# A fused Sinkhorn attention and SwiGLU kernel: a written order on PE, two-bank drains at the start, attention pieces between FFN steps, and unread matmuls in PE's gaps

## The chip, the cores and the metric

The kernel runs on one core of a Trainium2 chip. The metric is the device time of one execution in microseconds (us); smaller is better. The profile gives the span from the first to the last instruction, which is about 2 us shorter than the device time of the same run. Where two traces are compared, spans are used; where two kernels are compared, device times.

PE is the matmul engine, PEld its weight loads, DVE is VectorE, ACT is ScalarE, POOL is GpSimd. A drain is a copy that takes a matmul's result out of its PSUM bank. An unread matmul is one whose result nobody uses. The granted clock is the share of PE's full clock that the throttle allowed. Where several copies are quoted per copy, that is their busy time divided by their number: neighbouring records overlap, so the mean record on the page is longer.

## The reference

```python
B, H, S, D, n_blocks = 4, 8, 768, 64, 8          # block C = 96
P = sort_net                                       # (B, H, 8, 8)
for _ in range(5):                                 # Sinkhorn
    P = exp(P - max(P)); P /= P.sum(-1) ; P /= P.sum(-2)
k_sorted = einsum('bhij,bhjcd->bhicd', P, k_blocks)   # mix the 8 blocks
v_sorted = einsum('bhij,bhjcd->bhicd', P, v_blocks)
attn = softmax(q_block @ k_sorted.T / 8)           # 96 x 96 per block
x = (attn @ v_sorted)                              # as (3072 tokens, 512)
out = (silu(x @ w_gate) * (x @ w_val)) @ w_out     # 512 -> 1536 -> 512
```

Inputs and output are fp32; the kernel computes in bf16 with fp32 accumulation.

## The kernel before

A batch has eight attention units (two halves of the sequence times four pairs of heads). FFN works on a half of a batch (384 tokens) at a time, which I call a half-step: 12 gate and 12 value steps of 4 matmuls each, and an output projection of 3 x 12 matmuls. The parts that matter (cuts marked `# ...`):

```python
psum = ctx.enter_context(tc.tile_pool(name="psum", bufs=3, space=PSUM))   # one bank per tile

for it in range(5):                                # Sinkhorn: ScalarE and VectorE in turn
    nc.scalar.activation(p_sb, p_sb, AF.Exp)
    nc.vector.reduce_sum(...); nc.vector.reciprocal(...); nc.vector.tensor_mul(...)   # rows, columns
# ... the mix: lmix on VectorE, 16 small matmuls, products with masks

def emit_kq(b):                                    # mixes k, passes q: 12 chunks of 8 columns
    for cb in range(C // 8):
        tp = psum.tile([128, 8, 64], FP32, name="tkq", tag="att")
        for lc in range(8):
            for two in range(2):
                nc.tensor.matmul(tp[two * D:(two + 1) * D, lc, :], lhsT=nat[:, cb * 8 + lc, :],
                                 rhs=rm[:, two, :], start=True, stop=True)
        drain(dst[:, :, ts(cb, 8)], tp.transpose([0, 2, 1]))    # VectorE and ScalarE in turn

def emit_vch(pair):                                # transposes v's two free dimensions
    for s in range(4):                             # ... cs is the s-th quarter of the columns
        eng = nc.gpsimd if pair else nc.vector
        eng.tensor_copy(vch[:, :, cs], nat[:, cs, :].transpose([0, 2, 1]))

emit_att(0)
for b in range(B):
    if b + 1 < B:
        emit_att(b + 1)                            # all eight units of the next batch
    emit_gv(b, 0); emit_gv(b, 1); emit_out(b, 0); emit_out(b, 1)
```

The framework's scheduler orders the instructions of each engine and may mix these stages.

The softmax here doesn't subtract the row's maximum and nothing guards it: scores larger than these inputs give would overflow.

## Time and profile before

285.65 us (median of 4 runs, 285.48 to 286.93). The profiled execution took 287.63 us, so the spans and times of its trace below lie about 2 us above those of a median run.

| what | before |
|---|---|
| span | 285.9 us |
| PE's first matmul | 13.6 us |
| FFN dense from about | 46 us |
| PE busy | 257.2 us (90%) |
| granted clock, 36 to 49 us | 0.50 |

Lines of the profile's page, kernel before: busy times; then three rows of the span in 40 equal slices (7.15 us each), where a digit is a busy share, or granted PE clock, in tenths; then the chain of work that ended last.

```profile
PE 257.2 (90%) x2600; PEld 152.7 (53%) x2608; DVE 178.9 (63%) x383; ACT 121.7 (43%) x246; POOL 39.1 (14%) x51
...
PE   0077799969999999999999999999999999999993
...
ACT  2036745437633215976534215764332134343211
...
PEclk9999955979999999999999999999999999999999
...
PE 82%; DVE 11%; ACT 3%; issue 2%; ACTq 0%
```

PE bounds the kernel, but a busy digit doesn't say how much a busy PE gets done: the two 5s in the clock row are slices in which it is busy at least 90% of the time, at half speed. The timeline of PE in that stretch (start, duration, engine, line, operation, output<-inputs, shape, count) shows it:

```profile
36.09 0.51 PE L288 MATMUL g_ps<-xt,wg_sb 128*128 128x384 bf16 x1
36.39 0.52 PE L297 MATMUL v_ps<-xt,wv_sb 128*128 128x384 bf16 x1
36.71 0.52 PE L288 MATMUL g_ps<-xt,wg_sb 128*128 128x384 bf16 x1
37.30 0.50 PE L255 MATMUL x_ps<-ident,st 96*128 96x96 bf16 x4
```

Two starts of 384-column matmuls are 0.30 to 0.32 us apart; later in the trace they are 0.163 us apart (0.65 us for a step of four). The records overlap (0.51 us long, 0.30 us apart), so starts are compared throughout this text, not durations.

### The profile page before, as it was taken

How to read it: one execution, taken by the hardware profiler on the slowest of the kernel's cores; microseconds unless marked ns; L12 is line 12 of the kernel's file. 1: busy time of each engine (PE TensorE's matmuls, PEld its weight loads, DVE VectorE, ACT ScalarE, POOL GpSimd, SP SyncE). 2: the span in 40 equal slices, each digit the busy share in tenths (PEclk: the TensorE clock that was granted, in tenths of full speed). 3: DMA queues.
4: the chain of work that ended last, by engine and by line, in shares of the span. 5: the costliest groups of instructions: out<-in, count | busy, mean ns of one | idle time of the engine just before them, and what ended most of it. 6: DMA issues, size and time to landing. Idle time of an engine off the chain costs nothing.

```text
span 285.9 us, 6221 instructions
## 1 busy us (share of the span) xinstructions
PE 257.2 (90%) x2600; PEld 152.7 (53%) x2608; DVE 178.9 (63%) x383; ACT 121.7 (43%) x246; POOL 39.1 (14%) x51
## 2 busy tenths in 40 slices
PE   0077799969999999999999999999999999999993
PEld 0066555746655446666655446666555445555441
DVE  6798746937988205789988304699885018888300
ACT  2036745437633215976534215764332134343211
POOL 8557421029500000000000000000000000000000
PEclk9999955979999999999999999999999999999999
DMA  6999999999100122000000122000000220000021
GB/s 99 198 203 197 200 213 204 220 214 214 38 0 1 39 110 76 2 2 0 3 0 2 38 110 76 2 2 2 0 0 2 111 102 10 0 0 3 37 110 73
DMA packets 13659, 20.84 MB, mean 73 GB/s; under 512 B 1088, under 2 KB 8768, under 8 KB 13632
## 3 DMA queue, kind: packets, MB, share of 16 engines
q0 software_dynamic: 10128, 14.16, 28.2%
q1 hardware_dynamic: 3504, 6.30, 5.8%
q8 instruction: 20, 0.33, 0.4%
q14 instruction: 7, 0.06, 0.1%
HBM read 28.32 MB, written 6.29 MB: 121 GB/s over the span
## 4 chain that ended last, share of the span: by engine, by line
PE 82%; DVE 11%; ACT 3%; issue 2%; ACTq 0%
PE v_ps L297 22%; PE g_ps L288 22%; PE o_ps L308 22%; PE av_ps L245 4%; PE qk L230 4%; PE tkq L193 3%; PE x_ps L255 3%; PE tv L214 3%; DVE kqt L180 2%; DVE vch L204 1%; DVE st L251 1%; ACT vt L182 1%; DVE vt L180 1%; ACT th_sb L291 1%; DVE colred L136 0%
## 5 line engine op out<-in xcount | busy, mean ns | idle before, releaser
L288 PE MATMUL g_ps<-xt,wg_sb 128*128 128x384 bf16 x384 | 84.8, 331 | 0.2 <-DVE h L299 0.2
L297 PE MATMUL v_ps<-xt,wv_sb 128*128 128x384 bf16 x384 | 82.1, 331 | 0.0
L291 ACT ACTIVATE th_sb<-g_ps 128x384 bf16<-128x384 f32 x96 | 47.1, 491 | 63.2 <-PE g_ps L288 62.6
L293 DVE SCALAR_TENSOR_TENSOR gs_sb<-th_sb,g_ps 128x384 bf16<-128x384 bf16 x96 | 52.9, 551 | 26.9 <-ACT th_sb L291 20.9
L308 PE MATMUL o_ps<-wo_sb,h 128*128 128x512 bf16 x280 | 62.4, 379 | 0.4
L299 DVE SCALAR_TENSOR_TENSOR h<-v_ps,gs_sb 128x384 bf16<-128x384 f32 x96 | 53.1, 553 | 9.0 <-PE v_ps L297 0.8
L297 PEld LDWEIGHTS <-wv_sb 128*128 128x128 bf16 x384 | 36.8, 98 | 24.5 <-issue 0.8
L288 PEld LDWEIGHTS <-wg_sb 128*128 128x128 bf16 x384 | 36.2, 99 | 23.5 <-issue 2.3
L308 PEld LDWEIGHTS <-h 128*128 128x128 bf16 x288 | 28.2, 98 | 33.6
L180 DVE CAST kqt<-tkq 128x512 bf16<-128x512 f32 x24 | 15.9, 688 | 33.9 <-PE tkq L193 33.9
L311 ACT COPY o_sb<-o_ps 128x512 f32<-128x512 f32 x24 | 14.1, 586 | 51.4 <-PE o_ps L308 51.4
L235 ACT ACTIVATE er<-qk 96x384 bf16<-96x384 f32 x64 | 27.1, 487 | 12.2 <-PE qk L230 12.2
L193 PE MATMUL tkq<-rmix,kq 128*64 128x64 bf16 x768 | 20.3, 212 | 5.5 <-issue 2.5
L193 PEld LDWEIGHTS <-kq 128*64 128x64 bf16 x768 | 17.7, 126 | 8.9 <-issue 7.9
L251 DVE TENSOR_TENSOR st<-av_ps,r_sb 96x512 bf16<-96x512 f32 x32 | 21.9, 684 | 0.8
L182 ACT CAST kqt<-tkq 128x512 bf16<-128x512 f32 x24 | 14.1, 586 | 15.7 <-PE tkq L193 15.6
L230 PE MATMUL qk<-kqt 64*128 64x96 bf16 x256 | 14.0, 217 | 1.9 <-DVE kqt L180 1.4
L245 PE MATMUL av_ps<-vt,er 96*128 96x65 bf16 x256 | 14.9, 202 | 0.2 <-ACT vt L182 0.2
L180 DVE CAST vt<-tv 96x512 bf16<-96x512 f32 x16 | 12.2, 785 | 2.7 <-PE tv L214 2.5
L182 ACT CAST vt<-tv 96x512 bf16<-96x512 f32 x16 | 12.5, 787 | 2.1 <-PE tv L214 1.8
L214 PE MATMUL tv<-vmix,vch 128*128 128x128 bf16 x128 | 12.4, 236 | 1.0 <-DVE vt L180 0.3
L255 PEld LDWEIGHTS <-st 96*128 96x128 bf16 x128 | 7.6, 101 | 10.5 <-DVE st L251 9.1
(43 smaller groups left out, 123.0 us busy)
## 6 DMA issues: line engine op xcount, KB each, us to landing
out_dram<-o_sb SPq DMA_DIRECT2D x24, 256.0 KB, 2.0
v<-in_v_dram POOLq DMA_DIRECT2D x8, 384.0 KB, 13.1
kq<-in_k_dram POOLq DMA_DIRECT2D x6, 384.0 KB, 11.6
kq<-in_q_dram POOLq DMA_DIRECT2D x6, 384.0 KB, 12.1
wg_sb<-in_moe_w_gate_dram POOLq DMA_DIRECT2D x6, 256.0 KB, 11.8
wv_sb<-in_moe_w_val_dram POOLq DMA_DIRECT2D x6, 256.0 KB, 11.1
wo_sb<-in_moe_w_out_dram POOLq DMA_DIRECT2D x1, 1536.0 KB, 18.9
kq<-in_k_dram POOLq DMA_DIRECT2D x4, 192.0 KB, 5.6
```

Source lines behind the costliest of these rows:

```text
L180: nc.vector.tensor_copy(dst, src)
L182: nc.scalar.copy(dst, src)
L193: nc.tensor.matmul(tp[two * D:(two + 1) * D, lc, :], lhsT=nat[:, cb * 8 + lc, :], rhs=rm[:, two, :], start=True, stop=True)
L230: nc.tensor.matmul(pss[two][:, i4, :], lhsT=flat[lo:lo + D, at:at + 128], rhs=kqt[lo:lo + D, 1, g, i, :], start=True, stop=True)
L235: nc.scalar.activation(e[:, 0:4 * C], pss[two][0:C].rearrange("p a c -> p (a c)"), AF.Exp, scale=scale)
L245: nc.tensor.matmul(av[:, two, i4, :], lhsT=es[two][:, i4 * C:i4 * C + 128], rhs=vt[:, 2 * g + two, half * 4 + i4, :], start=True, stop=True)
L288: nc.tensor.matmul(g_ps, lhsT=wg_sb[:, kc, ts(m, 128)], rhs=xt[:, kc, :], start=(kc == 0), stop=(kc == NKC - 1))
L291: nc.scalar.activation(th_sb, g_ps, AF.Tanh, scale=0.5)
L293: nc.vector.scalar_tensor_tensor(gs_sb, th_sb, 1.0, g_ps, op0=ALU.add, op1=ALU.mult)
L297: nc.tensor.matmul(v_ps, lhsT=wv_sb[:, kc, ts(m, 128)], rhs=xt[:, kc, :], start=(kc == 0), stop=(kc == NKC - 1))
L299: nc.vector.scalar_tensor_tensor(h_w[:, m, :], v_ps, 0.5, gs_sb, op0=ALU.mult, op1=ALU.mult)
L308: nc.tensor.matmul(o_ps, lhsT=h_w[:, m, ts(t3, 128)], rhs=wo_sb[:, m, :], start=(m == 0), stop=(m == NFC - 1))
```

## The change

The intent: reach dense FFN work sooner, keep PE's clock up, and hide the attention of later batches between FFN steps. The diff is long (an almost new body); this is its core, with cuts marked `...`. First the order: the instructions of four engines stand as written in the start, those of PE and GpSimd for the rest.

```diff
+    man = tc.manual_schedule(engines={ET.PE, ET.Pool, ET.DVE, ET.Activation})
...
+    def copy_v(eng, pair, rows, s, n=4):
+        cs = slice(s * (C // n), (s + 1) * (C // n))
+        dst = vch3[rows, :, cs]
+        src = v_tiles[pair][rows, cs, :]
+        if eng is nc.scalar:
+            eng.copy(dst.transpose([0, 2, 1]), src)
+        else:
+            eng.tensor_copy(dst, src.transpose([0, 2, 1]))
...
     for it in range(N_ITER):
         nc.scalar.activation(p_sb, p_sb, AF.Exp)
...
+        if it == 2:
+            copy_v(nc.scalar, 0, lowr, 0, 8)
+            copy_v(nc.scalar, 0, lowr, 1, 8)
+        if it == 3:
+            copy_v(nc.scalar, 0, lowr, 2, 8)
+            copy_v(nc.scalar, 0, lowr, 3, 8)
...
+    for s in range(4, 8):
+        copy_v(nc.scalar, 0, lowr, s, 8)
```

Then the start on two-bank tiles, with unread matmuls (`fill`) between its four units:

```diff
+    for cb in range(6):                            # was 12 chunks of one bank
+        tp = pair_tile("tkq").rearrange("p (l n) -> p l n", n=2 * GI)
+        for lc in range(16):
...
+        drain("sv"[cb % 2], dst[:, :, ts(cb, 16)], tp.transpose([0, 2, 1]))
...
+    def fill(n):
+        warm(pair_tile("warm_ps")[:, 0:512], slice(0, 128), kqts[0][:, 0:512], n)
+
+    for u in range(4):
+        qk_wide(u)
+        fill(2)
+        if u >= 1:
+            av(0, u - 1, "pair")
+            fill(1)
...
```

Then the FFN stage: `merge` puts one attention piece after about every FFN step, in the order of the list, and an output projection comes one half-step after its gate and value steps. All k/q and v drains of this stage are on ScalarE ("s"), the drains of the transposes on VectorE ("v").

```diff
+    def kqs(b):
+        return [(0.34, lambda cb=cb: kq_chunk(b, cb, "s", "att")) for cb in range(12)]
...
+    merge(ffn(0), units(0, range(4, 8)) + kqs(1))
+    merge(ffn(1), [(0.28, lambda db=db: v_chunk(1, db, "s", "att")) for db in range(8)]
+          + units(1, range(4)))
...
+    merge(ffn(2), units(1, range(4, 8)) + kqs(2))
...
+    merge(ffn(4), units(2, range(4, 8)) + kqs(3))
+    merge(ffn(5), units(3, range(4)))
+    merge(ffn(6), units(3, range(4, 8)))
+    merge(ffn(7), [])
```

## The prediction

> **What bounds the kernel before.** PE: the chain of waits gives it 82% of the span. But there are two regimes.
>
> Steady state: the output projections of the four batches begin at 94.5, 159.0, 218.5 and 266.1 us (chain, in order of time). Warm rates from the timeline: gate or value step of 4 matmuls 0.65 us, output step of 4 0.87 us, qk 0.27, av 0.27, transpose 0.20 per unit, a k/q chunk 0.35. One batch of FFN is 48 x 0.65 + 18 x 0.87 = 46.9 us; the last period is 47.6 us, the one before 59.5 us for about 57 us of work. So it is already 96-99% dense; reordering it can win little.
>
> Start: the work done before 94.5 us is, at warm rates, about 31 us of gate/value plus 27 us of attention for batches 0 and 1, and PE's first matmul comes at 13.6 us. That would end at about 71 us: some 23 us are lost. Where (windows): one-bank drains and vch copies on VectorE alternate with PE from 14 to 33 us; a serial chain qk-exp-av-st-transpose of 2.5 us per unit at granted clock 0.50 from 36 to 49 us (a 384-column matmul takes 0.32 us instead of 0.16); an issue gap of 2.5 us at 57.4 us. The Trainium skill, "TensorE: Matmul & The Clock Gate", Part 1, says that the clock halves after an idle window and needs about 3.4 us of activity to return; this trace agrees (0.50 in 36-48 us, 1.00 from 51 us).
>
> **The change** loads only batch 0's v first, fuses the last Sinkhorn multiply with the mix, copies v on ScalarE inside Sinkhorn's gaps, drains two banks per instruction, runs only four of eight units before FFN, fills gaps with 25 unread 512-column matmuls, then spreads the rest between FFN steps.
>
> **Cost of the new start.** Sinkhorn rounds take 1.76 us: mix ready near 12.3 us, v products from about 13 us. Two-bank drains, estimated from the slope between 384 and 512 columns (ScalarE 478 to 586 ns): about 1.0 us ScalarE, 1.25 us VectorE; five on each, so k/q is ready at about 21.5 us (PE, cold at first, takes as long). Four units at about 2 us plus 2 us of pipeline end: first dense gate step at about 31.5 us.
>
> **The rest.** FFN 187.7 us, 28 units x 0.74 = 20.7, 36 k/q chunks = 12.4, v products about 5.8: 226.6 us. Stalls 6 us (2-3%): ScalarE now makes all k/q and v drains; half-step 3 has 16 v drains of 0.79 us beside tanh, locally more than PE's time; VectorE is tight in half-step 0. End as before, about 4 us. Sum: 31.5 + 226.6 + 6 + 4 = 268 us. Weights are no limit: 4.3 MB at about 200 GB/s, landed near 25 us.
>
> **Prediction: 268 us, 80% range 261 to 276.** Faster by over 2%: 0.93; within 2%: 0.06; slower: 0.01.
>
> **What would show it.** First gate matmul near 31.5 us (before: dense from 46); the slices' PEclk row without a 5 after 20 us; PE idle below 3% from there on; two-bank drains about 1.0/1.25 us; projections of the last half ending near 264 us.
>
> **What would make it wrong.** Clock lost in spite of the filling (10 us more); fillers or buffer rotation on the chain themselves (3 us); ScalarE copies delaying Sinkhorn; PE stalled behind ScalarE in half-steps 1 and 3 beyond 6 us; another issue gap while the DMA queues are full; or a shorter pipeline of four units (262 us).

## More of the kernel before

Note `emit_vch`: on VectorE, columns are innermost, so it writes runs of 24 neighbouring values.

The copy that will matter, from the groups of the profile by shape, kernel before: VectorE moves 1536 values per partition in 1.49 us.

```profile
L204 DVE COPY vch<-v 128x1536 bf16<-128x1536 bf16 x4 | 6.0, 1490 | 0.0
```

## The result

The changed kernel takes 303.99 us (median of 4 runs, 301.75 to 304.37) against 285.65 us: slower, by a ratio of 1.0615 (95% interval 1.0555 to 1.0675). A ratio here is the mean time of one kernel's fast runs over that of the other's of the same rounds, so it is not quite the ratio of the medians.

| what | before | after |
|---|---|---|
| span | 285.9 us | 302.5 us |
| v products begin | 25.6 us | 37.4 us |
| first dense gate step | about 46 us | 58.5 us |
| from there to the end | about 240 us | 244.0 us |
| ScalarE busy | 121.7 us | 159.2 us |

The page's lines, changed kernel, as before (slices of 7.56 us); the last is a group of the page's costliest: busy us and mean ns after the bar.

```profile
PE 257.4 (85%) x2675; PEld 146.3 (48%) x2697; DVE 154.6 (51%) x345; ACT 159.2 (53%) x261; POOL 40.8 (13%) x42
...
PE   0500087989999999999999999999999999999994
...
ACT  4999954454665544446499526355533244333321
...
PEclk9999996999999999999999999999999999999999
...
PE 77%; ACT 12%; DVE 6%; issue 2%; DMA 2%; ACTq 0%; POOLq 0%
...
L112 ACT COPY vch<-v 64x768 bf16<-64x768 bf16 x8 | 31.1, 4328 | 0.2 <-DMA v<-in_v_dram 0.2
```

The reader should see four things. PE is nearly idle in four of the first five slices; ScalarE is full from the second to the fifth; ScalarE's part of the chain that ended last rose from 3% to 12%; and eight copies of half the length of VectorE's old ones take 31.1 us together, 3.9 us each. The clock row has no 5 left, but a 6 from 45 to 53 us: the four units still ran at 0.50 until about 54 us, and from the first gate step on the granted clock is 1.00, which was one purpose of the change. The timeline of ScalarE, changed kernel, and then PE's first v products show how the copies reach the chain:

```profile
5.82 0.26 ACT L164 ACTIVATE p_sb<-p_sb 32x64 f32<-32x64 f32 x1 [1.51 <-DVE p_sb L182]
6.25 7.87 ACT L112 COPY vch<-v 64x768 bf16<-64x768 bf16 x2 [0.17 <-DMA v<-in_v_dram]
13.56 0.60 ACT L164 ACTIVATE p_sb<-p_sb 32x64 f32<-32x64 f32 x1
13.88 8.00 ACT L112 COPY vch<-v 64x768 bf16<-64x768 bf16 x2
21.29 0.60 ACT L164 ACTIVATE p_sb<-p_sb 32x64 f32<-32x64 f32 x1
21.61 15.71 ACT L112 COPY vch<-v 64x768 bf16<-64x768 bf16 x4
...
37.38 3.59 PE L377 MATMUL tv<-vmix,vch 64*128 64x64 bf16 x64 [13.03 <-ACT vch L112]
```

ScalarE takes its instructions in the written order. A gap in Sinkhorn is 1.5 us; two copies take 7.9 us, so the fourth and the fifth exp come 6 us late each, and then the last four copies hold the v products until 37.4 us.

What is left after the copies is smaller: from the first gate step to the end the changed kernel takes 244.0 us where the prediction had 236.6. PE's listed waits in that time are short (seven, 3.7 us together). The rest is inside "busy". Timeline of PE, changed kernel, half-step 0:

```profile
70.55 0.44 PE L213 MATMUL tkq<-rmix,kq 128*64 128x64 bf16 x16
70.93 0.82 PE L304 MATMUL g_ps<-xt,wg_sb 128*128 128x384 bf16 x4
71.68 0.44 PE L213 MATMUL tkq<-rmix,kq 128*64 128x64 bf16 x16
72.05 0.82 PE L317 MATMUL v_ps<-xt,wv_sb 128*128 128x384 bf16 x4
```

From start to start, the gate step takes 0.75 us instead of 0.65 us when a k/q chunk follows it, and the chunk takes 0.37 us. So there are two theories to test, for two sizes of loss.

- Theory A, for the 24 us: the copy's written order is what costs. It reads straight and writes each 2-byte value 192 bytes from the last. Rival B: ScalarE is slow in such copies whatever their order, or the loads in flight slow it.
- Theory S, for the 7 us: every entry from FFN matmuls into matmuls of another tile shape costs PE time. Rivals: the drains that were all put on ScalarE hold PE up (the prediction's reason for its 6 us of stalls), or queues on VectorE do.

### The profile page after: what moved, and what is told of

The parts are those of the page before. It is cut to its first block, busy times and chain, and to the rows that moved or that the text cites. A ratio compares the mean times of both kernels' runs of the same rounds, so it can differ in the third digit from the quotient of the medians.

```text
span 302.5 us, 6332 instructions
## 1 busy us (share of the span) xinstructions
PE 257.4 (85%) x2675; PEld 146.3 (48%) x2697; DVE 154.6 (51%) x345; ACT 159.2 (53%) x261; POOL 40.8 (13%) x42
## 4 chain that ended last, share of the span: by engine, by line
PE 77%; ACT 12%; DVE 6%; issue 2%; DMA 2%; ACTq 0%; POOLq 0%
PE o_ps L331 21%; PE v_ps L317 20%; PE g_ps L304 19%; ACT vch L112 10%; PE tkq L213 4%; PE qk L250 2%; PE av_ps L270 2%; DVE st L276 2%; DMA v<-in_v_dram 2%; PE x_ps L290 2%; PE tkq L387 2%; DVE gs_sb L309 1%; PE tv L377 1%; PE tv L235 1%; DVE h L319 1%
## 5 line engine op out<-in xcount | busy, mean ns | idle before, releaser
L304 PE MATMUL g_ps<-xt,wg_sb 128*128 128x384 bf16 x384 | 78.4, 326 | 0.1
L304 PEld LDWEIGHTS <-wg_sb 128*128 128x128 bf16 x384 | 33.5, 97 | 21.0 <-issue 0.6
L317 PEld LDWEIGHTS <-wv_sb 128*128 128x128 bf16 x384 | 33.6, 97 | 19.6
L195 ACT CAST kqt<-tkq 128x512 bf16<-128x512 f32 (+1 forms) x39 | 24.0, 616 | 15.7 <-PE tkq L213 12.6
L112 ACT COPY vch<-v 64x768 bf16<-64x768 bf16 x8 | 31.1, 4328 | 0.2 <-DMA v<-in_v_dram 0.2
L257 ACT ACTIVATE e_all<-qk 96x384 bf16<-96x384 f32 x56 | 24.3, 488 | 6.9 <-PE qk L250 6.9
L114 POOL COPY vch<-v 64x1536 bf16<-64x1536 bf16 (+1 forms) x8 | 22.2, 2827 | 28.8 <-DMA v<-in_v_dram 15.4
L195 ACT CAST vt<-tv 96x512 bf16<-96x512 f32 (+1 forms) x26 | 19.6, 783 | 6.2 <-PE tv L225 3.4
L213 PEld LDWEIGHTS <-kq 128*64 128x64 bf16 x576 | 11.9, 112 | 12.1 <-issue 12.1
L270 PEld LDWEIGHTS <-e_all 96*128 96x128 bf16 x256 | 12.7, 100 | 8.1 <-issue 2.7
L213 PE MATMUL tkq<-rmix,kq 128*64 128x64 bf16 x576 | 15.9, 199 | 0.0
L270 PE MATMUL av_ps<-vt,e_all 96*128 96x65 bf16 x256 | 13.9, 197 | 1.5 <-DVE st L276 1.4
L290 PE MATMUL x_ps<-ident,st 96*128 96x96 bf16 x128 | 10.9, 207 | 2.8 <-DVE st L276 2.7
```

What stands on the lines that cost most here:

```text
L112: eng.copy(dst.transpose([0, 2, 1]), src)
L195: nc.scalar.copy(dst, src)
L257: nc.scalar.activation(e[:, 0:4 * C], pss[two][0:C].rearrange("p a c -> p (a c)"), AF.Exp, scale=scale)
L270: nc.tensor.matmul(o[:, two, i4, :], lhsT=e[:, i4 * C:i4 * C + 128], rhs=vt[:, 2 * g + two, half * 4 + i4, :], start=True, stop=True)
L304: nc.tensor.matmul(g_ps, lhsT=wg_sb[:, kc, ts(m, 128)], rhs=xt[:, kc, :], start=(kc == 0), stop=(kc == NKC - 1))
L317: nc.tensor.matmul(v_ps, lhsT=wv_sb[:, kc, ts(m, 128)], rhs=xt[:, kc, :], start=(kc == 0), stop=(kc == NKC - 1))
```

## The experiments

Twelve more kernels ran. Each was timed in three rounds beside the kernel before, except `a3_measure`. All outputs are right.

| run | device time, median us | ratio to before, 95% interval | span us |
|---|---|---|---|
| changed kernel | 303.99 | 1.0615 (1.0555 to 1.0675) | 302.5 |
| a1_runs | 284.87 | 0.9958 (0.9924 to 0.9993) | 282.4 |
| a2_dve_strided | 302.31 | 1.0568 (1.0511 to 1.0625) | 299.9 |
| a3_measure | one look | | 302.0 |
| a4_runs_nofill | 284.83 | 0.9958 (0.9926 to 0.9990) | 282.9 |
| c1_pairs | 279.47 | 0.9750 (0.9687 to 0.9812) | 278.3 |
| c2_group | 274.25 | 0.9570 (0.9515 to 0.9624) | 272.3 |
| c3_turns | 283.46 | 0.9907 (0.9858 to 0.9956) | 281.3 |
| c4_twodrains | 280.34 | 0.9778 (0.9717 to 0.9839) | 278.5 |
| d1_space | 272.46 | 0.9529 (0.9489 to 0.9570) | 270.1 |
| d2_xt_act | 271.77 | 0.9498 (0.9445 to 0.9551) | 269.4 |
| d3_both | 269.81 | 0.9421 (0.9362 to 0.9479) | 268.6 |
| d4_fours | 276.49 | 0.9660 (0.9601 to 0.9720) | 274.2 |

### a1_runs: the same copies, columns innermost

```diff
-            eng.copy(dst.transpose([0, 2, 1]), src)
+            eng.copy(dst, src.transpose([0, 2, 1]))
```

> The changed kernel, with one line turned round: the eight v copies on ScalarE iterate columns innermost, so each writes runs of 12 neighbouring bf16 values and reads with a stride of 128 bytes, instead of reading straight and writing each value 192 bytes from the last. Theory A (the 3.9 us of a copy are the price of single-value strided writes): a copy falls to about 0.9 us, v products start near 13.5 us instead of 37.4, the kernel takes about 279 us. Rival B (ScalarE is slow in any such copy between SBUF places, or is slowed by the loads in flight): copies stay near 3.9 us and the kernel near 303 us.

Measured: 282.4 us of span, 20.1 us less than the changed kernel, from one line that moves the same bytes. v products begin at 18.1 us, the first gate step is at 38.4 us, and from there to the end it is 244.0 us, unchanged. Group of the profile by shape, `a1_runs`:

```profile
L112 ACT COPY vch<-v 64x768 bf16<-64x768 bf16 x8 | 11.4, 1486 | 0.4 <-DMA v<-in_v_dram 0.4
```

Theory A has the cause, and rival B falls as the main one. But a copy is 1.4 us, not the 0.9 that I expected, v products begin 4.6 us later than I expected for A, and the kernel (284.87 us) is 5.9 us behind the 279 us.

### a2_dve_strided: the same written order on VectorE

```diff
-        if eng is nc.scalar:
+        if n == 8:
             eng.tensor_copy(dst.transpose([0, 2, 1]), src)
...
-            copy_v(nc.scalar, 0, lowr, 0, 8)
+            copy_v(nc.vector, 0, lowr, 0, 8)          # all five calls
```

> The eight v copies in the same written order (single-value writes 192 bytes apart) and the same places, but on VectorE. If the order alone is slow (any engine pays): 3.9 us each and about 303 us again. If it is ScalarE's own slowness with it: about 0.9 us each; four of them delay Sinkhorn by about 3.5 us and four follow it, v products start near 19 us and the kernel takes about 285 us.

Measured: neither figure. VectorE takes 2.0 us a copy (16.0 us for eight), about half of ScalarE's time and twice what I expected of an engine without the trouble. So the order is slow on both, and slower on ScalarE. The kernel is hardly faster than the changed one (302.31 against 303.99 us) for a second reason, which I had not foreseen. First gate steps come at 50.1 us, 8.4 us earlier than there, but three small copies between SBUF tiles, 0.36 us together in the changed kernel, then hold VectorE, and from the first gate step to the end it takes 249.8 us instead of 244.0. Group by shape, then timeline of VectorE, `a2_dve_strided`:

```profile
L112 DVE COPY vch<-v 64x768 bf16<-64x768 bf16 x8 | 16.0, 2266 | 0.2 <-DMA v<-in_v_dram 0.2
...
49.18 7.32 DVE L427 COPY rmix<-ident 64x64 bf16<-64x64 bf16 x3
```

GpSimd is copying v at that time (busy 4.6 of 5 us from 45 to 50 us and all of the next 5; its last copy ends at 56.5 us, as VectorE's do). The Trainium skill, "SBUF — State Buffer", section "Who interferes with whom", says that VectorE and GpSimd share one pair of ports, that it is an exclusive lock, and that VectorE's copies are among the operations that can take it. This trace agrees (7.32 us for three copies against 0.36 us with GpSimd idle), while VectorE's drains out of PSUM in the same stretch kept their length (0.34 us for one). What PE lost in this run after 50 us is therefore no evidence on theory A.

### a3_measure: copies of each kind, after all loads

Ten unread copies of 64 x 768 values at the very end of the changed kernel, for example:

```diff
+    nc.scalar.copy(piece(0).transpose([0, 2, 1]), src)       # single-value writes
+    nc.scalar.copy(piece(1), src.transpose([0, 2, 1]))       # runs of 12
+    nc.scalar.copy(by(piece(2), 2, "p d (k r) -> p k d r"),  # runs of 2
+                   by(src, 2, "p (k r) d -> p k d r"))
...
+    nc.scalar.copy(flat[:, 0], late)                         # straight to straight
```

> The changed kernel plus, at its very end and after all loads, ten unread copies of 64 x 768 bf16: ScalarE with single-value strided writes, runs of 12, of 2, of 4, straight to straight, strided read to straight write; VectorE and GpSimd each with single-value writes and runs of 12. Theory A: ScalarE single-value writes again 3.9 us with no load in flight, runs of 2 about half of it, straight and strided-read copies about 0.8 us. Rival (contention with loads): the single-value copy at the end falls to about 0.8 us. The time of the kernel is not of interest.

Measured, groups of the profile by shape, `a3_measure` (L513 single-value writes, L515 runs of 12, L519 runs of 4, L523 strided read to straight write, L517 runs of 2, L521 straight, all on ScalarE; L525 single-value writes on VectorE):

```profile
L513 ACT COPY vch<-h 64x768 bf16<-64x768 bf16 x1 | 4.0, 4037 | 1.3 <-DVE h L319 1.3
L525 DVE COPY vch<-h 64x768 bf16<-64x768 bf16 x1 | 2.1, 2080 | 0.1
L515 ACT COPY vch<-h 64x768 bf16<-64x768 bf16 x1 | 1.7, 1715 | 0.0
L519 ACT COPY vch<-h 64x768 bf16<-64x768 bf16 x1 | 1.5, 1548 | 0.0
L523 ACT COPY flat<-h 64x768 bf16<-64x768 bf16 x1 | 1.5, 1492 | 0.0
L517 ACT COPY vch<-h 64x768 bf16<-64x768 bf16 x1 | 0.9, 926 | 0.0
L521 ACT COPY flat<-h 64x768 bf16<-64x768 bf16 x1 | 0.8, 841 | 0.0
```

Single-value writes take 4.04 us with no load in flight: contention with loads is out. The straight copy takes 0.84 us. The Trainium skill, "ScalarE: Activation LUTs", section "What ACT_TABLE_LOAD costs", has 186 ns plus 0.833 ns per element for an ACTIVATE with immediate scale and bias, which makes an estimate of 826 ns at 768; the straight copy agrees, the one with single-value writes is 4.9 times that figure. A strided read alone costs 1.49 us, which is why `a1_runs` fell short. Runs of 2 are almost free (0.93 us), against my expectation of half of 3.9 us, and runs of 4 are dearer than runs of 2: it is not simply that longer runs are better. The 1.72 us of runs of 12 are a little too long: that record overlaps by 0.56 us the single-value copy before it, and in `a1_runs` such a copy takes 1.43 us, its record 1.49 us. Writing pairs, the read alternates between two rows. The page "SBUF — State Buffer" says, in its note on cachelines, that at least two hits per 16-byte line are needed to run at full rate. For the writes this fits (one value a line 4.04 us, two 0.93 us), though a pair also fills a word of 4 bytes, and no run separates the two. For the reads it does not order these runs, and no run here says why.

The three engines copied side by side here. VectorE's single-value copy took 2.08 us, as in `a2_dve_strided` with GpSimd idle. Its copy in runs of 12 took 4.88 us beside a copy of GpSimd; by the lock above that figure says nothing of VectorE alone. GpSimd's own took 5.94 us with single values and 2.44 us in runs of 12, which for the same reason are no more than upper values.

### a4_runs_nofill: without the unread matmuls between the units

```diff
     def fill(n):
+        return
```

> As a1_runs, without the 16 unread matmuls between the four attention units of the start (the nine before the mix stay). If they keep the clock up: without them granted clock about 0.5 for several us after the units and the kernel 2 to 8 us slower than a1_runs. If they sit on PE's chain at half clock: the units end 2 to 3 us earlier and the kernel is that much faster.

Measured: both, and they cancel. The first gate step is at 36.7 us (38.4 with the filling), the span 282.9 against 282.4 us. Windows of the trace (us, busy time and count of PE, PEld, DVE, ACT and POOL, granted clock, DMA share, GB/s), first `a4_runs_nofill`, then `a1_runs`:

```profile
30.00:35.00 5.00, 4.52 (x60) 3.28 (x60) 3.47 (x11) 2.62 (x4) 0.00 (x0) 0.50 1.19 229
35.00:40.00 5.00, 3.84 (x25) 1.62 (x26) 1.48 (x6) 2.20 (x5) 0.00 (x0) 0.50 1.04 220
41.00:42.00 1.00, 1.00 (x11) 0.66 (x10) 0.00 (x0) 0.47 (x2) 0.00 (x0) 0.50 0.69 130
42.00:43.00 1.00, 1.00 (x16) 0.54 (x13) 0.76 (x3) 0.31 (x1) 0.00 (x0) 0.97 1.06 177
```

```profile
30.00:35.00 5.00, 5.00 (x55) 2.56 (x54) 2.15 (x7) 2.38 (x4) 0.00 (x0) 0.71 1.18 229
32.00:33.00 1.00, 1.00 (x16) 0.52 (x13) 0.56 (x2) 0.00 (x0) 0.00 (x0) 0.55 1.00 211
33.00:34.00 1.00, 1.00 (x18) 0.58 (x13) 0.37 (x2) 0.81 (x1) 0.00 (x0) 1.00 0.98 209
35.00:40.00 5.00, 4.37 (x51) 2.29 (x49) 2.60 (x10) 2.06 (x5) 0.00 (x0) 1.00 1.00 212
```

With the filling the clock is full some 9 us earlier (at 33 us instead of 42), and the first gate step comes 1.7 us later; from there to the end it is 244.0 instead of 246.2 us. In sum it is worth nothing here.

### c1_pairs: the copies in pairs of values

```diff
-            eng.copy(dst.transpose([0, 2, 1]), src)
+            eng.copy(dst.rearrange("p d (k r) -> p k d r", r=2), src.rearrange("p (k r) d -> p k d r", r=2))
```

> The changed kernel, with the ScalarE v copies written in pairs of neighbouring values (0.93 us for such a copy in a3_measure, against 1.72 for runs of 12 and 4.04 for single values). v products start near 14 us (a1_runs 18.1, changed kernel 37.4), first gate step near 34 us, span about 278 us. If the copies are slower while loads land than they were at the end of a3_measure: 1.2 to 1.5 us each and a span near 281 us.

Measured: a record of 0.91 us (0.85 us a copy), v products from 13.2 us, first gate step at 34.3 us, span 278.3 us, all as expected. Group by shape, `c1_pairs`:

```profile
L112 ACT COPY vch<-v 64x768 bf16<-64x768 bf16 x8 | 6.8, 908 | 0.1
```

That is 24.2 us less than the changed kernel, and 2.5% faster than the kernel before (1.9 to 3.1%). From the first gate step to the end it is again 244.0 us: the two losses are separate. The following kernels all stand on this one.

### c2_group: fewer entries into k/q and v matmuls

```diff
-        return [(0.34, lambda cb=cb: kq_chunk(b, cb, "s", "att")) for cb in range(12)]
+        def three(cb):
+            for c in range(cb, cb + 3):
+                kq_chunk(b, c, "s", "att")
+        return [(1.02, lambda cb=cb: three(cb)) for cb in range(0, 12, 3)]
...
-    merge(ffn(1), [(0.28, lambda db=db: v_chunk(1, db, "s", "att")) for db in range(8)]
+    merge(ffn(1), [(0.56, lambda db=db: (v_chunk(1, db, "s", "att"), v_chunk(1, db + 1, "s", "att")))
+                   for db in range(0, 8, 2)]
```

> As c1_pairs, but the k/q chunks stand between FFN steps in threes and the v chunks of half-step 1 in twos: the same work with 44 fewer to 16 entries from 128-row FFN matmuls into matmuls of other tile shape. If each entry costs PE about 0.1 us, as the starts of matmuls in the trace say (0.75 us for a gate step ahead of a chunk, 0.65 else): 2.8 us less than c1_pairs. If the excess of the half-steps is waiting for ScalarE and VectorE: no change, or slower by the burst of drains.

Measured: 272.3 us of span, 6.0 us less than `c1_pairs`; from the first gate step to the end 237.9 us. Theory S holds for the k/q and v chunks, at about twice the price I gave it. Timeline of PE, `c2_group`:

```profile
47.02 0.81 PE L317 MATMUL v_ps<-xt,wv_sb 128*128 128x384 bf16 x4
47.76 0.95 PE L213 MATMUL tkq<-rmix,kq 128*64 128x64 bf16 x48
48.65 0.82 PE L304 MATMUL g_ps<-xt,wg_sb 128*128 128x384 bf16 x4
49.30 0.81 PE L317 MATMUL v_ps<-xt,wv_sb 128*128 128x384 bf16 x4
```

Three chunks take 0.89 us from start to start, 0.30 each, where one alone took 0.37. With 0.10 us on the step before each entry, three chunks alone cost 3 x 0.47 = 1.41 us and a group of three 0.99 us. That is 0.42 us for two entries fewer, 0.21 us an entry, of which I had read only the 0.10. Twelve groups make 5.0 us, four v entries fewer about 0.8 us (a pair 0.57 us where two singles took 0.33 each, plus 0.10): together 5.8 of the 6.0 us. The price of 0.17 us in the expectation of `d4_fours` below came from an earlier, lower count of mine.

The profile has a sign of it. In the changed kernel the waits list has `PEld L213 <- issue: 12.1, 36, 0.4`: 36 times, once for each k/q chunk, the weight loads stood for a third of a us; in `c2_group` it is `PEld L213 <- issue: 4.0, 12, 0.4`, once for each group. The Trainium skill, "TensorE: Matmul & The Clock Gate", Part 2, says that PE pulls weight loads ahead of running matmuls when row groups don't conflict or the load goes to the background buffer. That this is what fails at a change of shape is my reading; the page does not say so and no run isolates it. The price goes with some shapes only. Entries into av and transposes (96 rows, 128 columns) and into the v chunks of half-step 3 (128 rows, 128 columns) show none: a gate step ahead of them takes 0.65 to 0.66 us. Entries into the v chunks of half-step 1 and into qk (64 rows, 128 columns) show it: 0.75 us. There are 28 entries into qk in every one of these kernels, about 2.8 us at 0.10 us each, which no run here tried to save.

### c3_turns: units and k/q chunks in turn (inconclusive)

```diff
-    merge(ffn(0), units(0, range(4, 8)) + kqs(1))
+    merge(ffn(0), turns(units(0, range(4, 8)), kqs(1)))     # also half-steps 2 and 4
```

> As c1_pairs, but in half-steps 0, 2 and 4 pieces of units and k/q chunks take turns, where c1_pairs has all units first. If half-step 0 is 4 us over its work because exps, tanhs and multiplies queue up while the units are close together: 2 to 3 us less than c1_pairs, with no wait for st above 0.3 us in that half-step. If the excess is the price of entries: no change.

Measured: slower than `c1_pairs`, 281.3 us, because of my own oversight. PE runs as written, and the first k/q chunk of batch 1 now stood ahead of its data. Timeline of PE, `c3_turns`:

```profile
40.40 0.64 PE L213 MATMUL tkq<-rmix,kq 128*64 128x64 bf16 x16 [5.29 <-DMA kq<-in_q_dram]
```

The wait is 5.3 us; the clock falls to 0.50 in it, at about 38.2 us, and is full again at 45.0 us. This run decides nothing between the theories. It shows that the load of batch 1 lands at about 40.4 us, and that a written order is only as good as its view of the loads.

### c4_twodrains: k/q and v drains on both engines

```diff
-kq_chunk(b, cb, "s", "att")
+kq_chunk(b, cb, "sv"[cb % 2], "att")        # the v chunks likewise
```

> As c1_pairs, but the k/q and v drains of the FFN stage alternate between ScalarE and VectorE, as the kernel before had them, where c1_pairs puts all on ScalarE. If ScalarE holds PE up in half-steps 1 and 3 (the prediction's reason for its 6 us of stalls): 1 to 3 us less than c1_pairs there. If not: no change or slightly slower.

Measured: 278.5 us against 278.3. The drains on ScalarE were not what held PE up; that reason of the prediction falls.

### d1_space, d2_xt_act and d3_both: the waits of half-step 0

Timeline of PE, `c2_group`; the bracket is PE's idle time and what ended it:

```profile
39.11 0.43 PE L270 MATMUL av_ps<-vt,e_all 96*128 96x65 bf16 x8 [0.58 <-DVE st L276]
43.91 0.42 PE L270 MATMUL av_ps<-vt,e_all 96*128 96x65 bf16 x8 [0.78 <-DVE st L276]
45.54 0.34 PE L290 MATMUL x_ps<-ident,st 96*128 96x96 bf16 x4 [0.39 <-DVE st L276]
86.24 0.34 PE L290 MATMUL x_ps<-ident,st 96*128 96x96 bf16 x4 [0.71 <-DVE st L276]
```

```diff
 # d1_space, and the same weight in half-steps 2 and 4
-    merge(ffn(0), units(0, range(4, 8)) + kqs(1))
+    merge(ffn(0), units(0, range(4, 8), 2.0) + kqs(1))
 # d2_xt_act
-                todo.append((0.2, lambda u=us[n - 2]: xtr(b, u, "v")))
+                todo.append((0.2, lambda u=us[n - 2]: xtr(b, u, "s")))
```

> As c2_group, with the unit pieces of half-steps 0, 2 and 4 spread wider between FFN steps (weight doubled). In c2_group PE waits for st three times in half-step 0 (0.58, 0.78, 0.39 us) and once near 86 us (0.71). If these are queues on VectorE and ScalarE because the units stand too close: the three waits go, about 1.5 to 2.5 us less than c2_group. If they are latencies of one unit that spacing doesn't hide: no change.

> As c2_group, with the drains of the transposes in the FFN stage on ScalarE (0.48 us) instead of VectorE (0.35 us). If VectorE's load is what the waits of half-step 0 come from (4.5 of 5 us busy there): 1 to 2 us less than c2_group. If ScalarE's exps and tanhs are: no change or 1 us more.

> d1_space and d2_xt_act together. If both take load off the same waits: as the better of the two, about 2 us less than c2_group; if they are separate: the sum, 3 us less.

Measured: spans 270.1, 269.4 and 268.6 us against 272.3. Part of these differences is the start, which nobody edited: the first gate step is at 33.6, 33.5 and 34.9 us against 34.4, early where the granted clock was full from about 28 us and late where it was full only from about 30 us. From the first gate step to the end the spans are 236.5, 236.0 and 233.8 us against 237.9. Spacing removed the waits of 0.58 and 0.78 us and left those of 0.71 and 0.46; moving the drain did the reverse (0.58 and 0.78 stay, the 0.71 is gone). With both, no wait of PE above 0.15 us is listed from the first gate step on. So these were queues on VectorE and ScalarE, in two places. With both, the 4.1 us saved after the first gate step are somewhat more than the sum of 1.4 and 1.9 us. The two runs alone are not clear of `c2_group` by their intervals; `d3_both` is, and it is the fastest kernel: 269.81 us, ratio 0.9421 to the kernel before.

### d4_fours: four chunks in a row, on two drain engines

```diff
-            for c in range(cb, cb + 3):
-                kq_chunk(b, c, "s", "att")
+            for c in range(cb, cb + 4):
+                kq_chunk(b, c, "sv"[c % 2], "att")
```

> As c2_group, with the k/q chunks in fours, drained by ScalarE and VectorE in turn, so 9 entries instead of 12. By the price of an entry, 0.17 us: 0.5 us less than c2_group. If three drain buffers don't carry four chunks in a row: PE waits inside a group and it is 1 to 3 us slower.

Measured: 274.2 us, 1.9 us slower than `c2_group`, and 3.0 us from the first gate step to the end (240.9 against 237.9 us). Timeline of PE, `d4_fours`:

```profile
47.28 0.95 PE L213 MATMUL tkq<-rmix,kq 128*64 128x64 bf16 x48
48.41 0.44 PE L213 MATMUL tkq<-rmix,kq 128*64 128x64 bf16 x16 [0.18 <-ACT kqt L195]
```

Three chunks fill the three drain buffers; the fourth begins 1.13 us after the first, where the three before it needed 0.89 us. The group of four ends 1.50 us after its start, more than one of three and one alone (0.89 + 0.37). Grouping pays up to the number of buffers. Two things were changed at once here, the size of a group and its drain engines; that the engines alone change nothing is from `c4_twodrains`.

## Why the prediction was wrong

The prediction had 268 us as the sum of four terms. Here they are against the changed kernel's trace (spans):

| term | predicted | measured | difference |
|---|---|---|---|
| v products begin | 13 us | 37.4 us | +24.4 |
| v products to first qk | 8.5 us | 10.8 us | +2.3 |
| four units, to the first gate step | 10 us | 10.3 us | +0.3 |
| first gate step to the end | 236.6 us | 244.0 us | +7.4 |
| sum | 268 us | 302.5 us | +34.4 |

**The step that failed is "Sinkhorn rounds take 1.76 us: mix ready near 12.3 us, v products from about 13 us".** The rounds without a copy did take 1.76 us. But the eight ScalarE copies were given no cost in it. The text says that they are made "inside Sinkhorn's gaps", and lists "ScalarE copies delaying Sinkhorn" only as a risk without a number. They took 3.9 us each where a gap is 1.5 us. That single-value writes are the reason is shown by `a1_runs` and `c1_pairs`, which change the order of the same copies and nothing else. The warning was in the diff: for ScalarE the transpose is on the destination, for the other engines on the source, and the only duration in the old trace was of the latter kind. With pairs (`c1_pairs`) the copies take 0.85 us, v products begin where the prediction had them (13.2 us), and the kernel is 24.2 us faster. This is shown.

**"36 k/q chunks = 12.4" and "Stalls 6 us".** The unit cost 0.35 us came from chunks that run in a row; alone among FFN steps, a chunk costs 0.37 us and 0.10 us of its neighbour, so 36 of them 16.9 us and not 12.4. The entries of 28 qk and 8 v chunks, at 0.10 us, make about 3.6 us more that no term had. The prediction held that reordering the steady state "can win little", and did not ask what it could lose. The reason given for the stalls, ScalarE's drains in half-steps 1 and 3, is wrong (`c4_twodrains`: no change). Entries into other tile shapes (6.0 us back with `c2_group`) and queues at the units (3.7 us more with `d3_both`) were in its place. PE's listed waits were 3.7 us where 6 us of stalls were allowed; 4.5 and 3.6 us more work and 2.3 us fewer stalls make 5.8 of the 7.4 us, an estimate from these starts, and the rest has no line.

**"k/q is ready at about 21.5 us".** The drains were sized right: 1.01 and 1.22 us measured for 1.0 and 1.25. A gap of 1.25 us, in which PE waits for nothing that the profile shows, fell in the middle. It comes after the 134th of these matmuls in every run with the new start, 0.9 to 1.6 us long (2.7 us in `a2_dve_strided`), while loads are in flight; the kernel before has one of 2.5 us at 57.4 us. No run tests its cause, but the traces have a strong hint. In each of the 14 traces a packet of 16 KB on the DMA queue that the profile names "instruction" begins 2.3 to 2.5 us before the gap ends (changed kernel: 43.21 and 45.68 us; kernel before: 57.49 and 59.90 us), wherever the gap begins. PE may have waited for its next instructions, which queue with the loads. Other such packets pass without a gap, so this is not shown.

**Right:** the four units (10 us predicted, 10.3 measured, partly by luck: the clock that the filling should keep was 0.50 from 48 to 54 us), the missing clock loss in FFN (1.00 from the first gate step on), PE idle below 3% from there to its last matmul (4.9 us of 240 us, 3.7 us of them in the seven waits), and that the weights are no limit. The last was right with a wrong size: 18 loads of 384 or 256 KB are about 5.5 MB, not 4.3. That slip cost nothing in the changed kernel, and would have warned me of the wait in `c3_turns`.

Of the two listed dangers of the filling, both are real and cancel (`a4_runs_nofill`).

On the clock, the prediction took the stretch of half clock in the old trace as a case of the rule that it cites. That stretch alone does not show the rule: PE's longest listed wait just before it is 1.0 us, and the profile calls PE busy for 12.76 of the 13 us. `c3_turns` is the clearer case: idle from 35.1 us, the clock at 0.50 from 38.2 us, working again from 40.4 us, full clock from 45.0 us.

## What to carry to other kernels

A copy's price is in its access pattern: before counting on a gap, find a duration of the same engine with the same operand strided, or measure it, and for 2-byte data write at least neighbouring pairs. Small pieces laid between long ones cost more than their own time where PE changes to tiles of 64 rows or columns, as here; group them up to the number of drain buffers. A PE that is busy 98% can still be slow, so compare starts of like steps and not busy shares.

## What the Trainium skill lacked or had wrong

- "ScalarE: Activation LUTs": the rate of one element per cycle is given without a condition on the write pattern. Here a ScalarE copy of 768 bf16 values takes 0.84 us straight, 0.93 us written in pairs, 1.49 us with a strided read and 4.04 us with single values written 192 bytes apart. For VectorE's 2.08 us in the last form I found no such figure in the notes either.
- "SBUF — State Buffer", note on cachelines: two hits per line as the threshold fits the writes (4.04 against 0.93 us), but it does not order the reads: runs of 4 (1.55 us) and of 12 (1.49 us in `a1_runs`) are slower than runs of 2 (0.93 us), whose reads change line at every value too.
- "TensorE: Matmul & The Clock Gate": the pull-ahead of weight loads is described, the price where the tile shape changes is not: about 0.21 us per entry from 128 x 128 tiles into 64-column ones here.
- "TensorE: Matmul & The Clock Gate", Part 1, advises against idle gaps. It gives no balance for filling them: here 16 unread 512-column matmuls brought the full clock about 9 us earlier, cost 1.7 us, and changed the total by nothing (ratio 0.9958 with and without).
- "Runtime: NRT & Kernel Launch", "Instruction fetch mechanics": no duration is given for a fetch of instructions that an engine has to wait for. The gap of 0.9 to 2.7 us on PE, which ends 2.3 to 2.5 us after a 16 KB packet of the instruction queue begins, may be one; no run here shows it.
